# Filter stages of a spectral layer: products issued for two frequency groups at a time, with PSUM slots of their own

## The chip, the core and the metric

The kernel runs on one core of a Trainium2 chip. That core has a matrix engine (TensorE, PE in the profile), a vector engine (VectorE, DVE), an activation engine (ScalarE, ACT), a general engine (GpSimd, POOL) and a queue engine that only issues transfers (SyncE, SP). Each engine works through its own list of instructions in order; a semaphore holds an instruction until what it needs is done. Matrix products land in PSUM, everything else on the chip lies in SBUF, and transfers go over 16 shared DMA engines. The metric is the time of one execution on the device in microseconds (us), as the median of several runs.

## The reference

Four residual layers run one after the other on x of 2048 positions by 576 features: attention over a sliding window of 256, a spectral filter, the same attention again, the same filter again.

```python
def _B_ref(x, w_r, w_i):
    X = jnp.fft.rfft2(x, axes=(-2, -1))
    X = X * (w_r + 1j * w_i)
    return jnp.fft.irfft2(X, s=(S, D), axes=(-2, -1))

x = A_x
x = x + _A_ref(_layernorm(x, axis=-1), A_wqkv, A_wo)
x = x + _B_ref(_layernorm(x, axis=-1), B_w_r, B_w_i)
x = x + _A_ref(_layernorm(x, axis=-1), A_wqkv, A_wo)
x = x + _B_ref(_layernorm(x, axis=-1), B_w_r, B_w_i)
```

The change touches the spectral layers only, and of them the middle part: the last step of the forward transform over positions, the multiplication by the filter, and the first step of the way back.

## The kernel before

Transforms are matrix products. A spectral layer (`layer_b`) turns the features first, then the positions. The 2048 positions are split as 16 times 128, so the transform over positions has two steps with a transfer through DRAM between them (`yd[0]` on the way in, `yd[1]` on the way back). Between the two transfers stands the filter stage. It runs over 16 groups of frequencies, g = 0 to 15; a group is a tile of 128 rows with a real and an imaginary half of 290 columns each. Per group:

- `g0` (line 451) loads the rows of two groups from `yd[0]`, issued on SP (L455). `gw` (L458) loads the filter weights of two groups where they are not there yet (L196).
- `g1m` (L462) is the forward product: four matrix products of 128 rows by 64 columns (L467; group 0 has four more, L469) into a PSUM tile called `p2_g` (in the profile `p`). Two of them fill the two halves of the columns of the matrix array at the same time. Then DVE multiplies that tile by the weights twice (L475, L476), and POOL takes the difference and the sum of these products into the two halves of `uv` (L478, L479).
- `g2` (L481) is the backward product: four matrix products of 64 rows by 128 columns (L488) into a PSUM tile `pq`; here two products use the two halves of the rows at the same time. Group 0 uses all 128 rows. Then ACT copies the tile to SBUF as `both` (L510), POOL takes the difference of the first 192 columns (L513), and DVE takes the sum (L514) and the rest of the difference (L515). The result, called `ze` in odd groups and `eo` in even ones, is stored to `yd[1]` (L525). ACT issues that store for all even groups up to 12 and for the odd ones up to 7; SP issues it for 9, 11, 13 and 15, POOL for 14.

From group 11 on the rows that the first tiles of the next stage need also go straight from SBUF to SBUF (`rows`, L495, mostly on SP), and SP reads back what was stored for earlier groups (L519). The first tiles of the next stage take these; the later ones are loaded whole from `yd[1]` (`ly`, L545), which waits for the stores. The next stage starts with the products `pi` (L551).

The whole program is scheduled by hand: what is written first is issued first on each engine. `pipe` (L620) runs its stages with a lag each: at step t it calls every stage on group t minus its lag, in the order of the list. In the filter stage that list is `[(10, g2), (7, g1m), (2, gw), (0, g0)]`, so at step t the backward product of group t-10 is followed by the forward product of group t-7.

PSUM holds four tiles of this size, in two pools of the class `Banks` (L118). Tiles with the tag "mm" take three of the slots in turn (`turn`); the fourth has the tag "tp" and serves transposes (L234) and warm-up products (L331). `uv` has three buffers, `both` two, the products p1 two and p2 three.

The layer is built twice, for the second and the fourth layer of the reference; `first` is true in the second one's code. Behind the filter stage the first one runs some products for the weights of the next attention layer (`w1`, `w2`), the last one 36 warm-up products (L536).

Of the kernel before, what the change touches and what calls it, by code (L numbers as in the profile page):

```python
# [8 lines left out]
F32 = mybir.dt.float32  # L9
# [108 lines left out]
class Banks:  # L118
# [6 lines left out]
    def tile(self, shape, dtype, tag, name, bufs):  # L125
        if tag != "mm":
            return self.pools[tag not in self.lower].tile(shape, dtype, tag=tag, name=name, bufs=bufs)
        self.turn = (self.turn + 1) % 3
        return self.pools[self.turn == 2].tile(shape, dtype, tag=tag, name=name, bufs=2 if self.turn < 2 else 1)

def layer_b(tc, xf, dst, dcs, gc, ident, rh, rl, out, ga_d, fc_d, m2_d, w_d, wo_d, wo2_d, dram, nxt, share):

# [9 lines left out]
    with ExitStack() as stack:  # L142
# [4 lines left out]
        pp = Banks(tc, banks, "bps", ())  # L147
# [13 lines left out]
        def ld(n2, h=None):  # L161
            if n2 % 2 == 0 and n2 not in xs:
                x = pairs[n2 // 2 % 4].rearrange("p (a d) -> p a d", a=2)
                nc.sync.dma_start(x, xfv[:, n2:n2 + 2])
                for q in range(2):
                    xs[n2 + q] = x[:, q].rearrange("p (c f) -> p c f", c=2)
# [174 lines left out]
        def w1(j, h=None, pool=None):  # L341
            turned(pool or wp, 16 + j, wos[j], wos[j]["eo"], wos[j]["tl"], "mm" if j == 4 else "tp")
# [11 lines left out]
        if first:  # L354
# [39 lines left out]
            ps = pp.tile([128, 2, 512], F32, tag="mm", name="opsb", bufs=3)  # L394
# [65 lines left out]
                pre_w(g // 2)  # L460

        def g1m(g, h):  # L462
            ps = pp.tile([128, 2, 512], F32, tag="mm", name=f"p2_{g}", bufs=3)

            for c in range(2):
                for j in range(2):
                    T.matmul(ps[64 * j:64 * j + 64, c, 0:NF], fc[:, g, j, c], h["y"][:, j], start=True, stop=g > 0)  # L467
                    if g == 0:
                        T.matmul(ps[64 * j:64 * j + 64, c, 0:NF], fc[:, 16, j, c], h["y"][:, 1 - j], start=False, stop=True)  # L469
            if g in (11, 13):  # L470
                ld(g - 11)
            w = wt[g]
            p1 = tws[g % 2]
            p2 = wp.tile([128, 2, NF], F32, tag="tc", name=f"p2_{g}", bufs=3)
            V.tensor_mul(p1, ps[:, :, 0:NF], w)  # L475
            V.tensor_mul(p2, ps[:, :, 0:NF], w[:, ::-1])  # L476
            h["uv"] = uv = ip.tile([128, 2, NF], F32, tag="ta", name=f"uv{g}", bufs=3)
            P.tensor_sub(uv[:, 0], p1[:, 0], p1[:, 1])  # L478
            P.tensor_add(uv[:, 1], p2[:, 0], p2[:, 1])  # L479

        def g2(g, h):  # L481
            pq = pp.tile([128, 2, 512], F32, tag="mm", name=f"pq{g}", bufs=3)
            uv = h["uv"]

            for c in range(2):
                for j in range(2):
                    r = slice(64 * j, 64 * j + 64) if g else slice(0, 128)
                    T.matmul(pq[:, j, 0:NF], m2[r, g if g or j == 0 else 16, c], uv[r, c], start=c == 0, stop=c == 1)  # L488

            ye = wp.tile([128, 2, NF], F32, tag="ye", name=f"ze{g}", bufs=NY) if g % 2 else eos[2 + g // 2 % 2 if first else g // 2 % 4]  # L490
            both = ip.tile([128, 2, NF], F32, tag="both", name=f"both{g}", bufs=2)
            zs[g] = yef = ye.rearrange("p c f -> p (c f)")

            def rows(eng, n2, k):
                eng.dma_start(yis[n2][8 * k:8 * k + 8].rearrange("p c f -> p (c f)"), zs[k][8 * n2:8 * n2 + 8])  # L495

            if g == 15:
                A.copy(both[:, 1], pq[:, 1, 0:NF])
                V.tensor_add(ye[:, 0], pq[:, 0, 0:NF], both[:, 1])
                V.tensor_sub(ye[:, 1], pq[:, 0, 0:NF], both[:, 1])  # L500
                if first:
                    w1(3)
                else:
                    rows(nc.scalar, 2, 13)
                    rows(nc.scalar, 2, 14)
                for n2 in range(near):
                    rows(nc.sync, n2, 15)
                held.pop()()
            else:
                A.copy(both, pq[:, :, 0:NF])  # L510
                if near > 2 and g in (FG + 1, FG + 2):
                    rows(nc.scalar, 2, g - 1)
                P.tensor_sub(ye[:, 1, 0:SH], both[:, 0, 0:SH], both[:, 1, 0:SH])  # L513
                V.tensor_add(ye[:, 0], pq[:, 0, 0:NF], both[:, 1])  # L514
                V.tensor_sub(ye[:, 1, SH:NF], pq[:, 0, SH:NF], both[:, 1, SH:NF])  # L515
            if g in (FG - 1, FG + 1):
                lo, hi = (0, 8) if g < FG else (8, FG)
                for n2 in range(near):
                    nc.sync.dma_start(yis[n2][8 * lo:8 * hi].rearrange("p c f -> p (c f)"), yd[1][n2, lo:hi].rearrange("g i f -> (g i) f"))  # L519
            if FG <= g < 15:  # L520
                for n2 in range(2):
                    rows(P if g == 14 and n2 else nc.sync, n2, g)

            def store():
                (P if g == 14 else nc.scalar if g < 13 and (g < 8 or g % 2 == 0) else nc.sync).dma_start(yd[1][:, g], yef)  # L525
            if g == 13:
                held.append(store)
            else:
                store()

        zs, held = {}, []
        pipe(16, [(10, g2), (7, g1m), (2, gw), (0, g0)])
        if first:
            w2(3)
        else:
# [84 lines left out]
def pipe(n, stages, behind=None):  # L620
    hold = [dict() for _ in range(n)]
    for t in range(n + max(l for l, _ in stages)):
        for lag, fn in stages:
            if 0 <= t - lag < n:
                fn(t - lag, hold[t - lag])
        if behind:
            behind(t)
# [799 lines left out]
```

## Time and profile before

| | |
|---|---|
| median of 3 runs | 1382.74 us (1381.52 to 1386.3) |
| the profiled execution's own time | 1389.17 us |
| span of its profile | 1387.4 us |
| TensorE busy | 1342.3 us of the span |
| VectorE / ScalarE / GpSimd busy | 893.1 / 786.9 / 638.6 us |
| first filter stage, first forward to last backward product | 607.13 to 645.42 us |
| second filter stage | 1272.99 to 1315.42 us |

The profile shows one execution. A row of its timeline has the start in us from the beginning of the span, the time it took, the engine, the line of the kernel, the operation, out<-in by the names of the program, the shapes, and how many instructions were merged into the row; in brackets stands how long the engine had been idle and what released it. PEld is the loading of weights into the matrix array, and a small q behind an engine's name (ACTq, SPq) marks work of its instruction queue, the issuing of transfers above all. A matrix product of this type is two instructions, so four products read x8. A busy TensorE is not TensorE at its peak, since its products are pipelined and their ends modelled.

### The profile page before, as it was taken

The page shows a single profiled execution, that of the slowest core. Times are in us where ns is not written, and L with a number is a line of the kernel's source. Part 1 is how long each engine was busy: PE and PEld are TensorE (multiplying, and loading weights), DVE is VectorE, ACT ScalarE, POOL GpSimd, SP SyncE. Part 2 cuts the span into 40 slices and gives each one's busy share as a digit, 9 for nine tenths or more (in the row PEclk, how much of TensorE's full clock was granted, in tenths as well). Part 3 has the DMA queues.
Part 4 walks back from the last instruction along what each step waited for, and adds up shares of the span by engine and source line. Part 5 has one row for each costly group of instructions (what it writes and reads, how often), then busy time and mean ns, then how long its engine had stood idle before and what let it go on. Part 6 is the DMA issues. An engine that isn't in the chain of part 4 may idle for free.

```text
span 1387.4 us, 33518 instructions
## 1 busy us (share of the span) xinstructions
PE 1342.3 (97%) x11330; PEld 1000.8 (72%) x11330; DVE 893.1 (64%) x3045; ACT 786.9 (57%) x1980; POOL 638.6 (46%) x1139
## 2 busy tenths in 40 slices
PE   7999999999999999998999999999999999998998
PEld 7986666666665699975999975666666655897577
DVE  5417777877778266666673157777778783564745
ACT  5622777777778544443355316777777778463223
POOL 2257555555547533475211394455545457102711
PEclk9999999999999999999999999999999999999999
DMA  6746555655446457678773467555554565497874
GB/s 199 203 151 205 190 185 175 190 163 161 147 150 187 109 158 242 218 239 265 247 229 76 110 198 231 166 165 165 163 160 136 159 171 157 162 349 249 259 226 157
DMA packets 202015, 259.09 MB, mean 187 GB/s; under 512 B 104254, under 2 KB 109630, under 8 KB 201334
## 3 DMA queue, kind: packets, MB, share of 16 engines
q1 hardware_dynamic: 191350, 235.63, 55.4%
q10 hardware_dynamic: 8000, 15.63, 3.3%
q0 software_dynamic: 2496, 5.71, 1.5%
q8 instruction: 91, 1.49, 0.4%
q14 instruction: 78, 0.64, 0.1%
HBM read 156.26 MB, written 101.01 MB: 185 GB/s over the span
## 4 chain that ended last, share of the span: by engine, by line
PE 46%; DMA 4%; ACT 2%; DVE 1%; issue 1%; SPq 1%; POOL 0%; ACTq 0%; DVEq 0%; POOLq 0%
PE pj L1021 9%; PE S L1078 6%; PE U L1135 6%; PE vps L958 4%; PE ops L758 4%; PE po L251 4%; PE E L1115 3%; PE pq L488 2%; PE p L467 2%; PE pi L551 2%; PE tpo L1149 1%; ACT P L1116 1%; DMA ofree<-yd 1%; PE pz L289 1%; SPq L495 1%
## 5 line engine op out<-in xcount | busy, mean ns | idle before, releaser
L1080 DVE CUSTOM_DVE_ANT_0 jk<-S,mask 128x384 bf16<-128x384 f32 (+2 forms) x1024 | 490.4, 529 | 110.0 <-PE E L1115 59.0
L1116 ACT ACTIVATE P<-E 128x384 f32<-128x384 f32 (+2 forms) x1024 | 408.9, 476 | 121.9 <-PE E L1115 98.2
L1118 POOL TENSOR_SCALAR_AFFINE_SELECT P<-P 128x512 f32<-128x512 f32 x256 | 162.7, 635 | 280.4 <-ACT P L1116 260.4
L1078 PE MATMUL S<-ks,qs 63*128 63x384 f32 (+2 forms) x1024 | 269.7, 372 | 0.6 <-DVE m L1080 0.4
L1115 PE MATMUL E<-qs,ks 64*128 64x384 f32 (+2 forms) x1024 | 222.1, 372 | 3.0 <-ACT P L1116 2.5
L1078 PEld LDWEIGHTS S<-ks,qs 63*128 63x128 f32 x1024 | 140.7, 185 | 105.7 <-DVE m L1080 72.2
L1135 PE MATMUL U<-P,vq 128*19 128x128 f32 (+1 forms) x3840 | 187.8, 328 | 1.0 <-ACT us L1140 1.0
L1021 PE MATMUL pj<-xh,wqh 128*128 128x512 f32 x360 | 156.5, 435 | 2.8 <-DVE sg L1036 1.5
L1135 PEld LDWEIGHTS U<-P,vq 128*19 128x19 f32 x3840 | 95.7, 98 | 77.5 <-issue 21.3
L1121 POOL TENSOR_SCALAR_AFFINE_SELECT P<-P 128x512 f32<-128x512 f32 x224 | 142.4, 636 | 0.0
L1115 PEld LDWEIGHTS E<-qs,ks 64*128 64x128 f32 x1024 | 113.9, 185 | 17.0 <-ACT P L1116 7.9
L1021 PE MATMUL pj<-xh,wql 128*128 128x512 f32 x360 | 124.5, 419 | 0.3 <-POOL wql L648 0.3
L1021 PE MATMUL pj<-xl,wqh 128*128 128x512 f32 x288 | 122.2, 424 | 0.0
L758 PE MATMUL ops<-oroom 128*128 128x290 f32 (+1 forms) x812 | 116.5, 300 | 0.2
L758 PEld LDWEIGHTS ops<-oroom 128*128 128x128 f32 x812 | 111.6, 191 | 0.7 <-DVE ofree L781 0.7
L1021 PEld LDWEIGHTS pj<-xh,wqh 128*128 128x128 f32 x360 | 68.0, 189 | 34.1 <-issue 10.4
L1036 DVE TENSOR_TENSOR sg<-pj,sg 128x512 fp32r<-128x512 f32 x72 | 49.5, 687 | 57.8 <-ACT sg L1033 57.8
L1080 DVE DVE_READ_ACCUMULATOR2_ANT m<- 128x1 f32 x1024 | 85.2, 83 | 0.0
L1021 PEld LDWEIGHTS pj<-xh,wql 128*128 128x128 f32 x360 | 64.2, 189 | 20.9 <-issue 10.7
L1033 ACT CAST sg<-pj 128x512 fp32r<-128x512 f32 x72 | 42.2, 586 | 61.6 <-PE pj L1021 46.1
L243 ACT CAST et<-tp 128x512 fp32r<-128x512 f32 x53 | 31.2, 588 | 76.9 <-PE tp L239 76.1
L958 PE MATMUL vps<-wvh,xh 128*128 128x288 f32 x320 | 72.1, 307 | 0.1
(221 smaller groups left out, 2298.5 us busy)
## 6 DMA issues: line engine op xcount, KB each, us to landing
qk_d<-sg SPq DMA_DIRECT2D x56, 512.0 KB
qs<-qk_d SPq DMA_DIRECT2D x384, 72.0 KB
ks<-qk_d SPq DMA_DIRECT2D x348, 72.0 KB
v_d<-vt SPq DMA_DIRECT2D x32, 304.0 KB
vq<-v_d SPq DMA_DIRECT2D x16, 608.0 KB
wt<-in_w SPq DMA_DIRECT2D x16, 580.0 KB
ofree<-x SPq DMA_DIRECT2D x16, 580.0 KB
x<-ofree SPq DMA_DIRECT2D x32, 290.0 KB
```

What stands on the lines that cost most here:

```text
L251: T.matmul(ps[:, c, 0:NF], tail[r] if si == 4 else hl_(si), dcs[b // 2][r, b % 2], start=mi == si == 0, stop=si == 4)
L758: self.nc.tensor.matmul(self.ps[u][n][:, 0:self.n], x, self.w[p][:, (2 * wk + n) * self.n:(2 * wk + n + 1) * self.n], start=first and i == ...
L958: T.matmul(ps[:, n, 0:288], xT(xk, c), w[:, wk, n * 288:(n + 1) * 288], start=i == 0, stop=i == len(ks) - 1)
L1021: T.matmul(box["ps"].rearrange("r (n p) -> r n p", n=NT) if second else box["ps"], w[:, wk], x, start=s == 0, stop=s == len(ks) - 1)
L1036: V.tensor_sub(rest[:, 1], by, rest[:, 0].bitcast(F32))
L1078: T.matmul(ps[:, 0:N], q[b:b + 63, pair, i * 128:i * 128 + 128], k[b:b + 63, pair, lo:hi], start=True, stop=True)
L1080: V.tensor_tensor_reduce(out=jk[:, 0:N], in0=ps[:, 0:N], in1=mask[:, 384 - N:384], scale=1.0, scalar=-3e38, op0=ALU.add, op1=ALU.max, accu ...
L1115: T.matmul(ps[:, 0:nq], k[b:b + 64, pair, j * 128:j * 128 + 128], q[b:b + 64, pair, j * 128:j * 128 + nq], start=True, stop=True)
L1116: A.activation(p[:, hl_, 0:nq], ps[:, 0:nq], AF.Exp, scale=SC)
L1118: P.affine_select(out=p[:, :, 0:128], in_=p[:, :, 0:128], pattern=[[0, 4], [1, 128]], compare_op=ALU.is_ge, fill=0.0, base=0, channel_mult ...
L1121: P.affine_select(out=p[:, :, 256:384], in_=p[:, :, 256:384], pattern=[[0, 4], [-1, 128]], compare_op=ALU.is_gt, fill=0.0, base=0, channel ...
L1135: T.matmul(U[32 * h:32 * h + 19, (q0 % 4) * 128:(q0 % 4) * 128 + 128 * (q1 - q0)], vts[n][:, j, h], pt[n, j][:, h, (q0 - j) * 128:(q1 - j) ...
```

## The change

The forward products of groups 2m and 2m+1 are issued together, then the backward products of groups 2m-2 and 2m-1, and so on. The function `both_` does that: it is called on every group, does nothing for an even one, and for an odd one calls the stage for the even group before it and then for itself. The forward list stands at lag 7 and the backward one at lag 9, so that a pair's backward products come one pair of forward products after its own. Loads keep their lags (0 and 2), through `one`. The list of dictionaries `filt` replaces the one in `pipe`, since a call now works on two groups.

Each kind has PSUM slots of its own. `slot(k, name)` gives slot 0 or 1 of the first pool for forward products (`g % 2`), and of the second pool the "mm" slot for odd backward products and the "tp" slot for even ones (`3 - g % 2`). All four slots are thus used in the filter stage, where it was three before. Instructions, shapes and data are the same; only their order and their PSUM addresses change.

```diff
@@ class Banks
         self.turn = (self.turn + 1) % 3
-        return self.pools[self.turn == 2].tile(shape, dtype, tag=tag, name=name, bufs=2 if self.turn < 2 else 1)
+        return self.slot(self.turn, name)
+
+    def slot(self, k, name):
+        self.turn = min(k, 2)
+        return self.pools[k > 1].tile([128, 2, 512], F32, tag="tp" if k == 3 else "mm", name=name, bufs=2 if k < 2 else 1)
@@ g1m
-            ps = pp.tile([128, 2, 512], F32, tag="mm", name=f"p2_{g}", bufs=3)
+            ps = pp.slot(g % 2, f"p2_{g}")
@@ g2
-            pq = pp.tile([128, 2, 512], F32, tag="mm", name=f"pq{g}", bufs=3)
+            pq = pp.slot(3 - g % 2, f"pq{g}")
@@ the call of pipe
-        pipe(16, [(10, g2), (7, g1m), (2, gw), (0, g0)])
+        both_ = lambda fn: lambda g, h: [fn(k, filt[k]) for k in (g - 1, g)] if g % 2 else None
+        filt = [dict() for _ in range(16)]
+        one = lambda fn: lambda g, h: fn(g, filt[g])
+        pipe(16, [(7, both_(g1m)), (9, both_(g2)), (2, one(gw)), (0, one(g0))])
```

The lines of the changed kernel lie four further down (L467 is L471, L488 is L492, L510 is L514, L525 is L529). On TensorE the first filter stage begins so before; `p2_3` is the forward tile of group 3, `pq1` the backward tile of group 1, and the number behind the underscore only tells tiles apart:

```order
L467 MATMUL p2_2_9780<-ofree_6984,fc_8097 64x290 x4
L488 MATMUL pq0_9791<-uv0_9765,m2_8098 128x290 x4
L467 MATMUL p2_3_9802<-ofree_6984,fc_8097 64x290 x4
L488 MATMUL pq1_9814<-uv1_9776,m2_8098 128x290 x4
L467 MATMUL p2_4_9826<-ofree_6984,fc_8097 64x290 x4
L488 MATMUL pq2_9837<-uv2_9788,m2_8098 128x290 x4
L467 MATMUL p2_5_9848<-ofree_6984,fc_8097 64x290 x4
L488 MATMUL pq3_9862<-uv3_9810,m2_8098 128x290 x4
```

And now, from the same place:

```order
L471 MATMUL p2_2_9780<-ofree_6984,fc_8097 64x290 x4
L471 MATMUL p2_3_9791<-ofree_6984,fc_8097 64x290 x4
L492 MATMUL pq0_9802<-uv0_9765,m2_8098 128x290 x4
L492 MATMUL pq1_9813<-uv1_9776,m2_8098 128x290 x4
L471 MATMUL p2_4_9826<-ofree_6984,fc_8097 64x290 x4
L471 MATMUL p2_5_9837<-ofree_6984,fc_8097 64x290 x4
L492 MATMUL pq2_9848<-uv2_9788,m2_8098 128x290 x4
L492 MATMUL pq3_9859<-uv3_9799,m2_8098 128x290 x4
```

Forward and backward blocks alternated one by one; now they alternate by twos. VectorE has the same order: the four products of a pair of groups, then sum and difference of the even backward tile, then of the odd one.

On GpSimd the same stretch, with the semaphores that each instruction waits for in brackets, was this before (`uv` are the sums of the products, `ze` and `eo` the differences of the backward tiles):

```order
L478 TENSOR_TENSOR uv4_9834<-ofree_6984 128x290 [waits DVE_49]
L479 TENSOR_TENSOR uv4_9834<-p2_4_9831 128x290 [waits DVE_49]
L513 TENSOR_TENSOR eo3_8102<-both2_9842 128x192 [waits Activation_49]
L478 TENSOR_TENSOR uv5_9856<-ofree_6984 128x290 [waits DVE_49]
L479 TENSOR_TENSOR uv5_9856<-p2_5_9853 128x290 [waits DVE_49]
L513 TENSOR_TENSOR ze3_9867<-both3_9868 128x192 [waits DMASW3_49,DMASW4_49,DMASW2_49,Activation_49]
```

Now it is this:

```order
L482 TENSOR_TENSOR uv4_9834<-ofree_6984 128x290 [waits DVE_49]
L483 TENSOR_TENSOR uv4_9834<-p2_4_9831 128x290 [waits DVE_49]
L482 TENSOR_TENSOR uv5_9845<-ofree_6984 128x290 [waits DVE_49,PE_49]
L483 TENSOR_TENSOR uv5_9845<-p2_5_9842 128x290 [waits DVE_49]
L517 TENSOR_TENSOR eo3_8102<-both2_9853 128x192 [waits Activation_49]
L517 TENSOR_TENSOR ze3_9864<-both3_9865 128x192 [waits DMASW3_49,DMASW4_49,DMASW2_49,Activation_49]
```

The difference of the even backward tile has moved behind the sums of the odd group, and those wait for TensorE as well: with three buffers, `uv5` lies where `uv2` lay, which the backward product of group 2 reads.

On ScalarE nothing has moved. Copies of the backward tiles and the stores of the results alternate as they did; in the changed kernel these rows read:

```order
L514 COPY both0_9807<-pq0_9802 128x580 [waits DVE_49,PE_49,Activation_49]
L529 DMA yd1_8081<-eo2_8101 16x8x580 [waits DMAHW0_49,DVE_49,Pool_49]
L514 COPY both1_9819<-pq1_9813 128x580 [waits PE_49,Activation_49]
L529 DMA yd1_8081<-ze1_9818 16x8x580 [waits DMAHW1_49,DVE_49,Pool_49]
L514 COPY both2_9853<-pq2_9848 128x580 [waits PE_49,Activation_49]
L529 DMA yd1_8081<-eo3_8102 16x8x580 [waits DMAHW4_49,DVE_49,Pool_49]
```

The store of an even group waits for VectorE and GpSimd and stands ahead of the copy of the odd group; what has changed is where the instructions that it waits for stand on their engines.

## The prediction

> **What bounds the kernel now.** I read the page's busy times first, then the busy times by stage, then the timelines of the engines in the filter stages, then the chain of waits behind them.
>
> ```profile
> PE 1342.3 (97%) x11330; PEld 1000.8 (72%) x11330; DVE 893.1 (64%) x3045; ACT 786.9 (57%) x1980; POOL 638.6 (46%) x1139
> 617.10:640.17 23.07, 23.07 (x162) 11.75 (x162) 19.63 (x41) 6.43 (x10) 18.47 (x31) 1.00 0.92 315
> ```
>
> The second row is ten groups of the first filter stage: length, busy us of PE, PEld, DVE, ACT and POOL, granted clock, DMA share, GB/s. PE never stops, DVE is busy for 19.63 of 23.07 us, POOL for 18.47. PE is the bound, the two behind it are close.
>
> ```profile
> 609.14 2.17 PE L467 MATMUL p<-ofree,fc 128*64 128x290 f32 x16
> 611.25 2.22 PE L488 MATMUL pq<-uv,m 128*128 128x290 f32 x8
> 613.40 1.20 PE L467 MATMUL p<-ofree,fc 128*64 128x290 f32 x8
> 614.53 1.25 PE L488 MATMUL pq<-uv,m 64*128 64x290 f32 x8
> 615.71 1.20 PE L467 MATMUL p<-ofree,fc 128*64 128x290 f32 x8
> ...
> 611.41 0.75 DVE L476 TENSOR_TENSOR p<-p,wt 128x580 f32<-128x580 f32 x1
> 614.77 0.75 DVE L475 TENSOR_TENSOR ofree<-p,wt 128x580 f32<-128x580 f32 x1
> 615.44 0.75 DVE L476 TENSOR_TENSOR p<-p,wt 128x580 f32<-128x580 f32 x1
> 616.55 0.46 DVE L514 TENSOR_TENSOR ze<-pq,both 128x290 f32<-128x290 f32 x1 [0.36 <-ACT both L510]
> 617.10 0.75 DVE L475 TENSOR_TENSOR ofree<-p,wt 128x580 f32<-128x580 f32 x1
> 640.17 0.75 DVE L475 TENSOR_TENSOR ofree<-p,wt 128x580 f32<-128x580 f32 x1
> 646.39 0.45 DVE L500 TENSOR_TENSOR ze<-pq,both 128x290 f32<-128x290 f32 x1
> ...
> 616.27 0.70 POOL L479 TENSOR_TENSOR uv<-p 128x290 f32<-128x290 f32 x1
> 616.92 0.52 POOL L513 TENSOR_TENSOR ze<-both 128x192 f32<-128x192 f32 x1
> ...
> 615.88 0.64 ACT L510 COPY both<-pq 128x580 f32<-128x580 f32 x1 [1.69 <-PE pq L488]
> 617.48 0.58 ACTq L525 DMA_DIRECT2D yd<-ze  x1
> 638.27 0.53 ACTq L525 DMA_DIRECT2D yd<-eo  x1
> ```
>
> See the steps. On PE, a forward block alone takes 1.13 us (613.40 to 614.53), a backward one 1.18 (to 615.71). On DVE the products start 0.67 apart, and from the first product of one group (617.10) to that of the group ten later (640.17) it is 23.07 us: 2.307 a group, 4.61 a pair. The others follow at fixed distances, which I use below.
>
> **The change: what it removes.** Two forward blocks in a row took 2.11 us (609.14 to 611.25), 0.15 less than twice 1.13, so each change of kind costs PE about 0.15. A stage has 27 such changes before and 13 after: 14 times 0.15 is 2.1 us, 4.2 for both stages. This is a gain only while PE is the bound.
>
> **What it adds: a loop through ACT's queue.** ACT's list is unchanged: copy of the even backward tile, its store, copy of the odd tile. The store waits for DVE and POOL. These now do the pair's four products and four half sums first. If the odd copy can't pass the waiting store, it waits for all that, and DVE, in order, has the odd tile's sum ahead of the next pair's products. Whether a waiting transfer holds a copy is seen at the end of the second stage, where ACT has one such transfer more:
>
> ```profile
> 644.54 0.64 ACT L510 COPY both<-pq 128x580 f32<-128x580 f32 x1 [0.34 <-PE pq L488]
> ...
> 1314.45 0.69 ACTq L495 DMA_DIRECT2D ofree<-eo  x1
> 1315.24 0.64 ACT L510 COPY both<-pq 128x580 f32<-128x580 f32 x1 [1.03 <-PE pq L488]
> 1315.78 0.41 ACT L498 COPY both<-pq 128x290 f32<-128x290 f32 x1
> ```
>
> In the first stage the copy of group 14 comes after 0.34 us of idling; in the second a transfer stands between, is issued until 1315.14, and the copy comes 0.10 later, after 1.03. It was held, through the issue too.
>
> [...]
>
> Now the loop, from the first product of pair (2m, 2m+1) at time M. The fourth product starts at M+2.00 (3 times 0.67). POOL's second half sum of the odd group starts 0.83 later (615.44 to 616.27): M+2.83. Its difference of the even tile follows 0.65 later (to 616.92) and lasts 0.52: M+4.00. The store starts 0.04 later (617.48), takes 0.53 (row 638.27), and the copy follows after 0.10: M+4.67. DVE's sum starts 0.67 after the copy (615.88 to 616.55), the next products 0.55 after that (to 617.10): **M+5.89**. Against 4.61 that is +1.28 a pair. PE needs 4.61 less two changes of kind, 4.31, so it idles 1.6 us in each pair; DVE's own work is 3.8 (4 times 0.67, twice 0.55), and neither is the bound. What is late is always the odd copy.
>
> The first stage in three parts. *Opening:* forward tiles have two slots, so group 3's waits until group 1's second product has ended, 611.41 plus 0.75, and starts at 612.25 instead of behind pq0. Plus 1.13 and the 2.15 of pq0 (611.25 to 613.40), seen 0.17 later (615.71 to 615.88), it is 615.7. The odd sum `uv3` lies in `uv0`'s buffer, so it starts then; 0.67 + 0.65 + 0.52 + 0.04 + 0.53 + 0.10 + 0.67 + 0.55 later group 4's products start: 619.4, where it was 617.10, **+2.3**. In later pairs the buffer of `uv` costs nothing: the backward product that reads it is over well before M. *Loop:* five steps from pair (4, 5) to (14, 15), 5 times 1.28, **+6.4**. *Closing:* with M the last pair's, the tile of group 13 is read out at M+5.9. Only then its slot takes the last backward block (1.18, seen 0.17 later); the copy of half a tile (0.41, row 1315.78) and two sums (0.46 and 0.45, a little overlapped) end at M+8.5. Before it was 640.17 to 646.84, 6.67: **+1.8**. So the last result stands 10.5 us later, at 657.3.
>
> What of this reaches the end is set behind the stage:
>
> ```profile
> 644.08 0.75 SPq L519 DMA_DIRECT2D ofree<-yd  x2
> 648.51 1.30 SPq L495 DMA_DIRECT2D ofree<-ze  x2
> 650.49 3.95 DMA yd<-ze
> 654.58 3.65 DMA ofree<-yd
> 658.36 2.27 PE pi L551 x4
> 664.86 0.98 PE pi L551 x4
> 668.38 0.98 PE pi L551 x4
> ```
>
> SP works through row transfers without a pause from 644.08, released by the landing of group 10's store (issued 638.27, 5.81 before). It comes to those of group 15 at 648.51, 1.67 after they were ready. Then come the last stores, their landing (3.95), a load (3.65), and PE goes on at 658.36. After the change the rows are ready at 657.3; SP is free then too (group 10's store at 647.0, plus 5.81, plus the 4.43 from 644.08 to 648.51). The rows go out at 657.4 instead of 648.51, and PE goes on **8.9** later. Against it stands the clock:
>
> ```profile
> 131.74:135.15 3.41, 1.94 (x10) 0.97 (x9) 1.86 (x6) 1.85 (x4) 1.76 (x3) 0.99 0.54 173
> 653.98:657.39 3.41, 1.49 (x13) 1.28 (x11) 0.69 (x1) 1.50 (x3) 0.57 (x3) 0.99 0.77 230
> 1271.80:1275.21 3.41, 2.22 (x18) 1.69 (x20) 0.00 (x0) 0.00 (x0) 0.00 (x0) 1.00 0.38 97
> ```
>
> After a stretch of 3.41 us with PE busy for 1.49, PE's tiles ran slow: 6.50 us from 658.36 to the next `pi`, where the following take 3.52, a loss of 3.0. After the change PE leaves the stage 10.6 later (656.0 for 645.42) and this wait ends 8.9 later, so the stretch before it is fuller and the clock may hold: 0 to -3.0. I take **-1.5**, the middle, since nothing here decides it. First stage: +7.4, between 5.9 and 8.9.
>
> The second stage:
>
> ```profile
> 1280.58 2.90 PE L488 MATMUL pq<-uv,m 128*128 128x290 f32 x8
> 1283.41 0.95 PE L467 MATMUL p<-ofree,fc 128*64 128x290 f32 x6
> 1287.11 0.75 DVE L475 TENSOR_TENSOR ofree<-p,wt 128x580 f32<-128x580 f32 x1
> 1308.26 0.53 ACTq L525 DMA_DIRECT2D yd<-eo  x1
> 1315.21 1.46 SPq L519 DMA_DIRECT2D ofree<-yd  x2
> 1316.83 0.45 DVE L500 TENSOR_TENSOR ze<-pq,both 128x290 f32<-128x290 f32 x1
> 1320.75 1.30 SPq L495 DMA_DIRECT2D ofree<-ze  x2
> ```
>
> Its loads come late, so no slot delays group 3; it starts in pq0's place at 1280.58. That block took 2.83 us instead of 2.15, 0.68 of a slow clock that now falls on group 3. So 1.13 + 0.68 + 2.15 + 0.17 and the same 3.73 of steps: 1288.4, **+1.3** against 1287.11. With 5 steps and the closing the last result stands at 1288.4 + 29.45 + 8.5 = 1326.4, where it was 1317.28. But SP came to its rows at 1320.75 only. If they now wait for nothing else, it is +5.7. If group 10's store, now at 1316.05, needs 6.95 us to free SP as before (1308.26 to 1315.21) and SP then the same 5.54, it is 1328.5, +7.8. With the first stage's 5.81 it is +6.7, which I take, since the slower loop asks less of the DMA engines (0.92 busy now).
>
> Sum: 7.4 + 6.7 = **14.1 us**, between 11.6 and 16.7. On the profiled execution's 1389.17 (span 1387.4) that is 1403.3, 1.0% more. That execution lay 0.5% above the median of the runs; on the median of 1382.74 it is **1396.8**. Loads, weights and x are issued on SP for pairs three ahead and have more time than now: nothing.
>
> **Rivals.** *Copies pass waiting stores.* Then PE stays the bound and the fewer changes of kind give 4.2 us. The opening takes back 1.0 in the first stage (groups 2 and 3 wait 0.7 and 0.3 for their slots, which without them would start at 610.1 and 611.9 instead of 610.8 and 612.25), and SP behind the stages, late already, swallows a part: between 0 and -3.2, I say -2, 1380.7. It decides from the point where an odd copy starts within 0.2 us of its backward block's end. Row 1315.24 speaks against it, the shorter forward blocks for it. [...]
>
> *A copy passes the store's issue but not its wait.* It would then start 0.63 earlier (0.53 + 0.10), in 7 pairs of each stage: 8.8 less, +5.3, 1388.0. The same row is against it, since there the copy waited for the issue too.
>
> *The clock falls in the loop.* The rows above say that 1.94 busy of 3.41 lost the clock and 2.22 kept it. In the loop PE is busy 4.31 of 5.89, and around its longest gap (1.1 and 0.3) about 2.0 of 3.41, between them. One fall costs 1.7 us at most and hides in the 1.6 idle of a pair; lasting, 8.6 a pair, 2.7 more in 12 pairs: +33 on top, 1429. At half speed PE is busy all the time, which speaks against lasting.
>
> *The ends swallow more.* If the landings and loads behind the stages (7.6 us in the first, about as much in the second) get shorter by 2 each, and both lower bounds hold, it is 11.6 - 4 = +7.6, 1390.3.
>
> **How the numbers follow.** The likeliest has 0.71, with 1394.3 to 1399.4 as its own range; the two rivals on ACT's queue 0.08 each, the clock 0.05, the ends 0.08. The range reaches from 1390, the ends' case, to 1401, the upper bound with a little of the clock's. A measurement of this kernel tells 0.3% (4 us) from nothing. Faster by more comes only from the first rival's upper half, 0.04; no change from its rest and some of the second, 0.05; slower is 0.91.
>
> **What would show it.** In the profile after: odd copies on ACT start 0.10 behind the store of the even group, 4.67 after the pair's first product; those first products lie 5.89 apart; PE idles about 1.6 a pair, ended by ACT, DVE or POOL; two blocks of a kind take 2.1. The stages last about 49 and 52 us instead of 38.3 and 42.4. Wrong it would be if odd copies start right behind their products on PE, or if the distance is near 4.3.

## The result, and the profile after

The changed kernel takes 1404.33 us (median of 5 runs, 1401.2 to 1405.13), the kernel before 1381.92 (median of 5, 1379.59 to 1386.3): a ratio of 1.0148, 95% interval 1.0132 to 1.0164. A second measurement, shown below, gave 1.0135 (1.0109 to 1.0162). It is slower, as forecast, but by more than forecast: 1396.8 was a ratio of 1.0102, and the upper end of the range, 1401, one of 1.0132.

The two profiled executions took 1389.17 and 1405.13 us, 16.0 apart; 14.1 was forecast for them. Where it went is read in the same order as before: busy times, then the stretch of five pairs in each filter stage (length, busy us of PE, PEld, DVE, ACT and POOL, granted clock, DMA share, GB/s).

```profile
PE 1343.9 (96%) x11330; PEld 1002.3 (71%) x11330; DVE 891.6 (64%) x3045; ACT 786.5 (56%) x1980; POOL 639.2 (46%) x1139
618.72:648.43 29.71, 24.39 (x166) 13.21 (x162) 19.17 (x41) 6.97 (x11) 18.63 (x31) 1.00 0.75 229
1296.02:1325.72 29.70, 24.45 (x166) 13.16 (x162) 19.18 (x41) 6.97 (x11) 18.62 (x31) 1.00 0.76 231
```

The work is the same, the length is not: ten groups take 29.71 us where they took 23.07. TensorE is busy for 24.4 of it, and no engine for more. That is the mark of a loop from engine to engine, in which each waits for the next. TensorE idles in two gaps, 1.08 us a pair (0.19 and 0.89). Here is one turn of it, by the timelines of PE, DVE, POOL and ACT (start, time taken; in brackets the idle time before and what ended it):

```profile
620.24 1.20 PE L471 MATMUL p<-ofree,fc 128*64 128x290 f32 x8
621.62 1.20 PE L471 MATMUL p<-ofree,fc 128*64 128x290 f32 x8 [0.19 <-DVE p L480]
622.75 1.25 PE L492 MATMUL pq<-uv,m 64*128 64x290 f32 x8
624.89 1.25 PE L492 MATMUL pq<-uv,m 64*128 64x290 f32 x8 [0.89 <-DVE ze L519]
...
618.72 0.75 DVE L479 TENSOR_TENSOR ofree<-p,wt 128x580 f32<-128x580 f32 x1
620.72 0.75 DVE L480 TENSOR_TENSOR p<-p,wt 128x580 f32<-128x580 f32 x1
624.12 0.46 DVE L518 TENSOR_TENSOR ze<-pq,both 128x290 f32<-128x290 f32 x1 [2.11 <-ACT both L514]
624.66 0.75 DVE L479 TENSOR_TENSOR ofree<-p,wt 128x580 f32<-128x580 f32 x1
...
621.61 0.70 POOL L483 TENSOR_TENSOR uv<-p 128x290 f32<-128x290 f32 x1
622.26 0.53 POOL L517 TENSOR_TENSOR eo<-both 128x192 f32<-128x192 f32 x1
...
622.82 0.53 ACTq L529 DMA_DIRECT2D yd<-eo  x1
623.44 0.64 ACT L514 COPY both<-pq 128x580 f32<-128x580 f32 x1 [3.24 <-PE p L471]
```

From M = 618.72: fourth product M+2.00, second half sum of the odd group M+2.89, difference of the even tile M+3.54 to M+4.07, store M+4.10, copy of the odd tile M+4.72, its sum M+5.40, next products M+5.94. Forecast were 2.00, 2.83, 3.48, 4.00, 4.04, 4.67, 5.34 and 5.89. The copy begins 0.09 behind the store's issue, after ScalarE had idled 3.24, and the backward block that it reads had ended by 620.28 (618.05 plus 2.23), 3.16 us before. Whether the store ahead of it is what holds it is tried below.

The closing of the first stage (PE, then DVE):

```profile
648.66 1.25 PE L492 MATMUL pq<-uv,m 64*128 64x290 f32 x8 [0.89 <-ACT both L514]
651.87 2.31 PE L492 MATMUL pq<-uv,m 64*128 64x290 f32 x8 [1.96 <-DVE eo L519]
654.61 2.30 PE L492 MATMUL pq<-uv,m 64*128 64x290 f32 x8 [0.43 <-DVE ze L519]
...
648.43 0.75 DVE L479 TENSOR_TENSOR ofree<-p,wt 128x580 f32<-128x580 f32 x1
654.21 0.25 DVE L519 TENSOR_TENSOR ze<-pq,both 128x98 f32<-128x98 f32 x1
657.80 0.45 DVE L504 TENSOR_TENSOR ze<-pq,both 128x290 f32<-128x290 f32 x1
```

The last two backward blocks took 2.3 us each instead of 1.25: in the gap before them, for the even tile's read-out, TensorE's clock had fallen to half. In the second stage it fell later, and only the last block was slow (1329.16 and 1331.90 below). The windows show it as the granted clock, the third figure from the end:

```profile
647.96:651.38 3.42, 1.25 (x8) 0.78 (x8) 3.42 (x7) 0.56 (x1) 2.58 (x5) 1.00 0.40 107
651.38:658.20 6.82, 5.90 (x22) 3.74 (x22) 2.37 (x8) 1.68 (x3) 3.24 (x6) 0.50 0.55 136
658.20:661.61 3.41, 2.73 (x21) 2.58 (x21) 0.74 (x2) 1.26 (x3) 0.00 (x0) 1.00 0.44 108
1327.21:1330.63 3.42, 1.25 (x8) 0.78 (x8) 1.80 (x4) 0.18 (x1) 2.54 (x5) 1.00 0.57 143
```

The clock fell at 651.38 and 1330.63, each time behind 3.41 us with TensorE busy for 1.25. In this profile and in the first one of before the changes of the granted clock lie whole multiples of 3.413 us apart (here 651.38, 658.20 and 1330.63; before 135.10, 657.34 and 664.17), but where they fall in the program differs between the two.

Behind the first stage and at the end of the second (PE, DVE, SP; `warm` are the 36 warm-up products):

```profile
668.00 1.22 PE L558 MATMUL pi<-ofree,ga 128*128 128x290 f32 x4 [1.59 <-DMA ofree<-yd]
671.60 1.14 PE L558 MATMUL pi<-ofree,ga 128*128 128x290 f32 x4
675.13 1.14 PE L558 MATMUL pi<-ofree,ga 128*128 128x290 f32 x4
1329.16 1.25 PE L492 MATMUL pq<-uv,m 64*128 64x290 f32 x8 [1.96 <-DVE eo L519]
1331.90 2.30 PE L492 MATMUL pq<-uv,m 64*128 64x290 f32 x8 [1.49 <-DVE ze L519]
1334.13 6.54 PE L337 MATMUL warm<-dc 128*128 128x290 f32 x36
1340.51 2.12 PE L558 MATMUL pi<-ofree,ga 128*128 128x290 f32 x8
1351.68 1.14 PE L558 MATMUL pi<-ofree,ga 128*128 128x290 f32 x4
...
1335.09 0.45 DVE L504 TENSOR_TENSOR ze<-pq,both 128x290 f32<-128x290 f32 x1
...
655.92 0.62 SPq L499 DMA_DIRECT2D ofree<-eo  x1
658.28 1.30 SPq L499 DMA_DIRECT2D ofree<-ze  x2
1333.22 0.62 SPq L499 DMA_DIRECT2D ofree<-eo  x1
1335.57 1.98 SPq L499 DMA_DIRECT2D ofree<-ze  x3
```

In both stages SP idles ahead of the last rows (658.28, 1335.57) and goes on right behind the last result (658.25, 1335.54). Before, it was SP that came late: 1.67 us after the rows were ready in the first stage. In the first stage the clock then held: 3.60 from 668.00 to the next `pi`, where it was 6.3 before (658.36 to 664.70). In the second the warm-up products began at half clock, took 6.54 us instead of 5.08 and pushed `pi` to 1340.51.

To compare executions I measure each stage from its first forward product: to the end of its last result, and to the fourth row of `pi` products, where TensorE runs undisturbed again (675.13 and 1351.68 here). This table is read from the same rows of all profiles; "pair" is the distance between the first products of two pairs, the mean of five:

| profile | pair | 1st stage: last result | 4th `pi` | 2nd stage: last result | 4th `pi` | ratio to before |
|---|---|---|---|---|---|---|
| before | 4.61 | 39.7 | 61.1 | 44.3 | 62.7 | |
| before, second profile | 4.61 | 39.7 | 60.4 | 43.2 | 60.8 | 0.9990 (0.9980 to 1.0001) |
| changed | 5.94 | 51.9 | 68.8 | 55.0 | 71.1 | 1.0148 (1.0132 to 1.0164) |
| changed, second profile | 5.94 | 51.9 | 68.7 | 53.4 | 69.6 | 1.0135 (1.0109 to 1.0162) |
| copies first | 4.26 | 39.9 | 59.4 | 43.8 | 61.8 | 1.0008 (0.9992 to 1.0024) |
| difference ahead | 5.20 | 47.0 | 63.9 | 48.6 | 63.9 | 1.0060 (1.0041 to 1.0080) |
| slots alone | 4.61 | 41.3 | 59.9 | 43.5 | 60.1 | 0.9998 (0.9985 to 1.0011) |
| order alone | 5.94 | 48.4 | 68.1 | 51.1 | 68.5 | 1.0103 (1.0077 to 1.0129) |
| late slots | 5.94 | 49.5 | 70.1 | 52.7 | 71.1 | 1.0121 (1.0097 to 1.0146) |
| all three | 4.26 | 39.4 | 60.5 | 43.3 | 61.6 | 1.0009 (0.9994 to 1.0024) |
| ends | 4.26 | 39.7 | 60.6 | 44.7 | 62.3 | 1.0008 (0.9996 to 1.0020) |
| before with ends | 4.61 | 39.7 | 58.1 | 43.0 | 60.3 | 0.9986 (0.9974 to 0.9999) |

Changed less before is 7.7 + 8.4 = 16.1 us by the first pair of profiles and 8.3 + 8.8 = 17.1 by the second. What lies outside these two stretches (span less both) is 1263.6 and 1263.5 in the first pair, and 1262.0 to 1266.3 over all twelve profiles, whatever the kernel. So the loss in these executions is in the two filter stages and what follows each.

### The profile page after: what moved, and what is told of

The parts are those of the page before. It is cut to its first block, busy times and chain, and to the rows that moved or that the text cites. A ratio compares the mean times of both kernels' runs of the same rounds, so it can differ in the third digit from the quotient of the medians.

```text
span 1403.4 us, 33528 instructions
## 1 busy us (share of the span) xinstructions
PE 1343.9 (96%) x11330; PEld 1002.3 (71%) x11330; DVE 891.6 (64%) x3045; ACT 786.5 (56%) x1980; POOL 639.2 (46%) x1139
## 4 chain that ended last, share of the span: by engine, by line
PE 72%; DMA 8%; POOL 4%; ACT 3%; DVE 3%; issue 3%; SPq 2%; ACTq 1%; DVEq 0%; POOLq 0%
PE pj L1028 16%; PE S L1085 11%; PE U L1142 10%; PE ops L765 7%; PE E L1122 5%; PE vps L965 4%; PE po L255 4%; PE pf L255 2%; PE tpo L1156 2%; PE pi L558 2%; ACT P L1123 2%; DMA ofree<-yd 2%; PE pz L293 2%; DMA qs<-mt 1%; DMA ks<-qk_d 1%
## 5 line engine op out<-in xcount | busy, mean ns | idle before, releaser
L1043 DVE TENSOR_TENSOR sg<-pj,sg 128x512 fp32r<-128x512 f32 x72 | 49.5, 687 | 58.3 <-ACT sg L1040 58.3
L1028 PEld LDWEIGHTS pj<-xh,wql 128*128 128x128 f32 x360 | 64.2, 189 | 20.9 <-issue 10.7
L1040 ACT CAST sg<-pj 128x512 fp32r<-128x512 f32 x72 | 42.1, 585 | 61.6 <-PE pj L1028 51.8
L247 ACT CAST et<-tp 128x512 fp32r<-128x512 f32 x53 | 31.1, 587 | 71.4 <-PE tp L243 71.2
```

The source lines that it names most:

```text
L1028: T.matmul(box["ps"].rearrange("r (n p) -> r n p", n=NT) if second else box["ps"], w[:, wk], x, start=s == 0, stop=s == len(ks) - 1)
L1043: V.tensor_sub(rest[:, 1], by, rest[:, 0].bitcast(F32))
```

## The experiments

**Copies first.** Theory: the store ahead of the odd copy closes the loop. Rival: pairing starves TensorE by itself.

```diff
                 A.copy(both, pq[:, :, 0:NF])
+                if late:
+                    late.pop()()
...
             if g == 13:
                 held.append(store)
+            elif g % 2 == 0 and g < 13:
+                late.append(store)
             else:
                 store()
```

> The changed kernel, with one instruction moved on ScalarE: the store of an even group up to 12 is issued behind the copy of the odd group instead of ahead of it. ScalarE's queue theory: the odd copy no longer waits for GpSimd's difference, the loop is gone, and TensorE is the bound again at 4.31 us a pair (4.61 less two changes of kind). The first products of a pair lie 4.3 to 4.5 apart instead of 5.94, and the last result of the first stage comes 39 to 41 us after the stage's start instead of 51.9; the time falls from 1404 to between 1378 and 1384. Rival, the pairing by itself starves TensorE (two forward slots, three buffers of uv, the order on GpSimd): the distance stays above 5 and the time above 1390. Rival, the copies were never held and the time went elsewhere: nothing changes, 1404.

Measured: 1388.73 us against 1387.1 of before, a ratio of 1.0008. The profile, one pair (PE, ACT) and the store of group 10:

```profile
618.79 2.17 PE L471 MATMUL p<-ofree,fc 128*64 128x290 f32 x16
620.90 2.23 PE L492 MATMUL pq<-uv,m 64*128 64x290 f32 x16
...
617.99 0.64 ACT L514 COPY both<-pq 128x580 f32<-128x580 f32 x1 [2.65 <-DVE ofree L479]
618.97 0.64 ACT L514 COPY both<-pq 128x580 f32<-128x580 f32 x1 [0.34 <-PE pq L492]
620.02 0.53 ACTq L531 DMA_DIRECT2D yd<-eo  x1
637.08 0.53 ACTq L531 DMA_DIRECT2D yd<-eo  x1
```

TensorE has no idle time left, the odd copy waits for nothing but its block, and a pair takes 4.26. One instruction moved in one queue takes nearly all of the loss back: the loop went through ScalarE's queue. The 0.35 us between 4.61 and 4.26 is the gain of two fewer changes of kind in a pair. Yet the kernel isn't faster than before, and the time missed what was expected (1378 to 1384): those bounds stood on before's 1382 us, and before measured 1387.1 beside this run; besides, they took for granted that the loop's gain reaches the time. From the last group's first product to the last result it takes 6.3 and 8.6 us, 4.4 and 5.0 in the second profile of before.

**Difference ahead.** GpSimd's order alone; ScalarE's queue stays as in the changed kernel.

```diff
+        def g1s(g, h):
+            uv, (p1, p2) = h["uv"], h["p"]
             P.tensor_sub(uv[:, 0], p1[:, 0], p1[:, 1])
             P.tensor_add(uv[:, 1], p2[:, 0], p2[:, 1])
...
+                do(g1m, g - 1)
+                do(g1s, g - 1)
+                do(g1m, g)
+                do(g2, g - 3)
+                do(g1s, g)
+                do(g2, g - 2)
```

> The changed kernel, with GpSimd's list alone in another order: the difference of the even backward tile stands ahead of the odd group's two sums instead of behind them. ScalarE's list is as in the changed kernel, store ahead of the odd copy. ScalarE's queue theory: the store then waits for VectorE's part of the even tile, which ends 0.77 before GpSimd's did (1299.31 against 1300.09), so the odd copy, the odd sum and the next products come 0.77 earlier: 5.17 us between the first products of two pairs instead of 5.94. With 5 steps, an opening and a closing in each stage that is about 5 us a stage, 1394 (1391 to 1397). Rival, the loop goes through PSUM slots, buffers or VectorE's own order: the distance stays at 5.94 and the time at 1404.

Measured: 1395.92 us, a ratio of 1.0060 where the changed kernel had 1.0135 to 1.0148. DVE, POOL and ACT:

```profile
624.67 0.75 DVE L479 TENSOR_TENSOR ofree<-p,wt 128x580 f32<-128x580 f32 x1
629.88 0.75 DVE L479 TENSOR_TENSOR ofree<-p,wt 128x580 f32<-128x580 f32 x1
...
626.83 0.53 POOL L521 TENSOR_TENSOR eo<-both 128x192 f32<-128x192 f32 x1
...
628.04 0.53 ACTq L533 DMA_DIRECT2D yd<-eo  x1
628.66 0.64 ACT L518 COPY both<-pq 128x580 f32<-128x580 f32 x1 [2.56 <-POOL uv L487]
```

The store stands at M+3.37 instead of M+4.10, and the distance falls by as much, from 5.94 to 5.20 on average. So the store's wait sets the loop, and in the changed kernel what it waits for last is GpSimd's difference. The time fell about as said: 0.0075 to 0.0088 of ratio is 10 to 12 us.

**Slots alone, order alone.** The two halves of the change.

```diff
-        pipe(16, [(7, both_(g1m)), (9, both_(g2)), (2, one(gw)), (0, one(g0))])
+        pipe(16, [(10, one(g2)), (7, one(g1m)), (2, one(gw)), (0, one(g0))])
```

> Half of the change: the slots of the changed kernel (two for forward products, one for odd and one for even backward products), with the order of before, one backward and one forward block in turn. If the order is what costs: the pairs lie 4.61 us apart as before, and the time is that of before within 0.3% (1378 to 1386). If the slots cost by themselves (a forward tile must wait for its own kind's slot): TensorE idles in the stage, and the time is 1388 or more.

```diff
-            ps = pp.slot(g % 2, f"p2_{g}")
+            ps = pp.tile([128, 2, 512], F32, tag="mm", name=f"p2_{g}", bufs=3)
...
-            pq = pp.slot(3 - g % 2, f"pq{g}")
+            pq = pp.tile([128, 2, 512], F32, tag="mm", name=f"pq{g}", bufs=3)
```

> The other half of the change: the pairs' order, with forward and backward tiles taking the three slots of before in turn. ScalarE's queue theory: the loop runs through the order only, so the distance between pairs is 5.9 to 6.0 us as in the changed kernel, and the ratio to before 1.012 to 1.018. Rival, one slot of its own for each kind matters: with three slots in turn the even backward block has to wait for the odd tile's read-out of the pair before, and if that adds to the loop the distance is over 6.3 and the ratio over 1.02; if on the other hand the slots of their own were the cost, the distance falls towards 4.6.

Slots alone: 1388.14 us, 0.9998, pairs of 4.61; nothing in the time. (The bounds of 1386 and 1388 were put on the earlier, lower base; before measured 1387.1 beside it.) Order alone: 1401.55 us, 1.0103, pairs of 5.94, the whole loop. The ratio came out below what was expected. With three slots in turn two things are cheaper: group 3's forward block doesn't wait for a slot of its kind (the last group's first product stands 42.3 us from the stage's start instead of 43.4), and the last four backward blocks follow each other without the gap of 1.96, at 4.90 us for the four:

```profile
647.11 4.90 PE L492 MATMUL pq<-uv,m 64*128 64x290 f32 x32 [1.14 <-DVE ze L519]
```

So under the order by pairs the slots of their own cost 3.5 us of the 12.2 by which the first stage's last result is late (51.9 less 48.4); under the order of before they cost 1.6 (41.3 against 39.7). Little of the 3.5 is seen at the fourth `pi`: 68.1 against 68.8. Whether that explains the whole of the lower ratio isn't shown.

**Late slots.** The closing alone.

```diff
-            pq = pp.slot(3 - g % 2, f"pq{g}")
+            pq = pp.slot(g % 2 if g > 13 else 3 - g % 2, f"pq{g}")
```

> The changed kernel, with the backward tiles of groups 14 and 15 in the two forward slots, which nobody uses any more by then. It tests the closing. Slot theory: the two last blocks no longer wait for the read-out of groups 12 and 13; with M the first product of the last pair, block 14 can start when its half sums are ready (M+2.2), block 15 at M+3.6 instead of M+6.18, TensorE's gap of 1.96 goes and with it the half clock of the last block. What is left is ScalarE's odd copy (M+4.7) and VectorE's six operations behind it: the last result at about M+7.7 instead of M+9.82, 2 us earlier in each stage, and in the second stage the 36 warm-up products run at full clock. 3 to 6 us less than the changed kernel, a ratio of 1.010 to 1.013. Rival, the closing is set by the copies alone: under 1 us in a stage and no change in the time.

Measured: 1403.52 us, 1.0121 against 1.0135 for the changed kernel beside it; the intervals overlap. PE, at the end of the first and of the second stage:

```profile
649.25 4.17 PE L492 MATMUL pq<-uv,m 64*128 64x290 f32 x24 [0.89 <-DVE ze L519]
668.28 1.54 PE L558 MATMUL pi<-ofree,ga 128*128 128x290 f32 x4 [3.01 <-DMA ofree<-yd]
673.50 1.14 PE L558 MATMUL pi<-ofree,ga 128*128 128x290 f32 x4
1339.11 4.21 PE L558 MATMUL pi<-ofree,ga 128*128 128x290 f32 x8 [3.24 <-DMA ofree<-ze]
```

Half of the expectation held. The last blocks run at full clock, and the last results come 2.4 and 2.3 us earlier. But the time is only 1.6 us less where 3 to 6 were expected, and in this profile nothing arrives: the fourth `pi` stands at 70.1 and 71.1. TensorE now waits longer for its rows, its clock falls in that wait or right behind it (5.22 us from 668.28 to the next `pi` instead of 3.60; 4.21 for the first two `pi` of the second stage instead of 2.12), and what the result gained the slow products lose. Late result and full clock, or early result and half clock: in these profiles the ends come out alike.

**All three, and the ends.** Do the pairs pay once the loop and the closing are mended? First, copies first and late slots together, with ScalarE's row transfers of groups 11 and 12 in the second stage moved behind the copies of 13 and 15.

```diff
-                if near > 2 and g in (FG + 1, FG + 2):
-                    rows(nc.scalar, 2, g - 1)
+                if near > 2 and g == 13:
+                    rows(nc.scalar, 2, 11)
...
-                    rows(nc.scalar, 2, 13)
-                    rows(nc.scalar, 2, 14)
+                    for k in (12, 13, 14):
+                        rows(nc.scalar, 2, k)
```

> Three edits of the changed kernel together: even stores behind the odd copies (as in the run with the copies first, which came to before's time), the tiles of groups 14 and 15 in the forward slots, and in the second stage ScalarE's row transfer of group 11 behind the copy of 13 and that of 12 behind the last copy. The loop is then 4.27 us a pair, below before's 4.61, and the closing, which took 6.3 and 8.6 us from the last product to the last result with the copies first against 4.4 and 5.0 before, should fall to 4 to 5.5. If SyncE's queue behind the stages lets it through, 2 to 4 us less than before, a ratio of 0.997 to 0.999; if SyncE's row transfers, ready at their own pace, decide the ends, the ratio is 0.999 to 1.001.

Measured: 1389.21 against 1386.67, a ratio of 1.0009. The closing was still 5.8 and 8.0 us, where 4 to 5.5 were expected. Then two edits behind the stage, on this kernel and on before (the store of 13 is no longer held back behind the rows of 15, either):

```diff
-                (P if g == 14 else nc.scalar if g < 13 and (g < 8 or g % 2 == 0) else nc.sync).dma_start(yd[1][:, g], yef)
+                (P if g > 12 else nc.scalar if g < 13 and (g < 8 or g % 2 == 0) else nc.sync).dma_start(yd[1][:, g], yef)
...
-            warm(36)
+            warm(60)
```

> The three edits together once more, and behind the stage two others: the stores of groups 13 and 15 are issued by GpSimd as soon as these are ready, not by SyncE behind the row transfers, and behind the second stage stand 60 warm-up products instead of 36. It tests what swallowed the gains of the stage. If it is the chain from SyncE's last store over its landing (about 4 us) to the load of the third tile, and TensorE's half clock behind a gap, then that load can start about 2 us earlier in each stage and the first pi products run at full clock: 60.5 and 61.6 us from the stage's start to the fourth pi row become 58 to 59.5 each, and the ratio to before 0.996 to 0.999. If SyncE's row transfers or the DMA engines themselves are the limit, nothing changes: 0.999 to 1.002.

> The kernel before with the same two edits behind the stage and no other: stores of 13 and 15 from GpSimd, 60 warm-up products. It tells what the pairs' order is worth once the ends let a gain through. If the ends are as said, this is faster than before by 1 to 4 us, a ratio of 0.997 to 0.999, and the kernel with pairs is faster than this one by what its loop saves, 1 to 3 us. If the two come out alike, the order by pairs is worth nothing even without its loop through ScalarE's queue.

Measured: 1388.77 us with pairs, 1.0008; 1385.61 without, 0.9986 (0.9974 to 0.9999). The second is the only version here whose whole interval lies below 1, and that barely: the kernel before, measured once more against itself, came out at 0.9990 (0.9980 to 1.0001). The kernel with pairs, expected 1 to 3 us ahead of it, is 3.2 us behind. In the first stage the loads do start earlier, but TensorE's first `pi` row waits for other rows and starts 45.3 us from the stage's start, with pairs, and 45.5 without. It then takes 4.21 us with pairs, at half clock, and 2.19 without, at full clock; the 2.5 us between the fourth rows (60.6 and 58.1) come behind it. SP, second stage of the kernel with pairs and ends:

```profile
1317.16 1.37 SPq L524 DMA_DIRECT2D ofree<-yd  x3
1318.63 1.34 SPq L499 DMA_DIRECT2D ofree<-eo  x2
1320.07 1.29 SPq L499 DMA_DIRECT2D ofree<-ze  x2
1321.48 0.78 SPq L499 DMA_DIRECT2D ofree<-eo  x1
1322.35 2.57 SPq L499 DMA_DIRECT2D ofree<-ze  x3
```

SP works without a pause from 1317.16 on, so the rows that `pi` needs are set by when it begins, not by the last result (1319.86). In the first stage of before and of the kernel with the copies first it begins when the store of group 10 has landed. With the copies first that store is issued 32.1 us from the stage's start (637.08 less 604.94) and SP begins at 37.8; before these were 31.1 (638.27 less 607.13) and 37.0. Counted from group 4's first product the store stands at 21.2 us in both: what the faster loop gains up to there is taken by its later place, behind two forward blocks and two copies. The 1.0 that is left is the longer opening (11.0 us instead of 10.0 to group 4's first product). So the gain of the pairs, 0.35 us each, isn't seen on the path that goes through this store. That this path is what keeps the gain from the time is argued from the rows, not tried, and which of the waits holds the second stage wasn't tried either.

**Both kernels once more.**

> The kernel before once more, for a second profiled execution. The first one's own time, 1389.2, lay 7 us above the median of the runs, and that of the changed kernel only 1 above its median; that is where most of the miss in the predicted difference could lie. If the 7 us were a disturbance of that one execution, the second has a span of 1378 to 1383, and the comparison by stretches shows where the first lost them; the two filter stages keep 38.3 and 42.4 us within 0.5. If a profiled execution of before is always that long, the span is again about 1387.

> The changed kernel once more, for a second profiled execution of it. From its start to the fourth row of pi products the first filter stage took 68.8 us and the second 71.1; in the two profiled executions of before these were 61.1 and 62.7, then 60.4 and 60.8. If before's first execution was the odd one, mainly in its second stage, this run repeats 68.8 and 71.1 within 1 us, and its ratio is again 1.013 to 1.017. If the changed kernel's stages vary as much, the second stage comes out 1.5 us or more off.

Before: 1385.5 us (12 runs, 1382.84 to 1388.94), the profiled execution 1388.94. Changed: 1405.13 (5 runs), the profiled one 1405.13. First stages repeat within 0.7 us. The second stage is 1.9 us shorter in before's second profile and 1.5 in the changed kernel's, both for 1.1 to 1.6 in the last result: its opening varies from one execution to the next, in both kernels. So neither expectation fits whole. The first profile of before wasn't odd in itself. The stages of two profiles compare to 2 us or so, whole executions less well: over the twelve profiles here the profiled execution lay between 4.3 us below and 7.3 us above the median of its kernel's runs.

## Where the prediction held, and which steps failed

The direction and the mechanism held; the size did not. 1396.8 us was forecast, 1401 at most, and 1404.33 measured, 7.5 more than the likeliest. Two steps failed. In the sum, the closing was too short, because the half clock was left out of it: with what followed it in the second stage, the sum came out 1.9 us low (14.1 for 16.0 between the profiles). The other 5.6 are the base: a sum worked out on one profiled execution was put on the median of before's runs. What lies behind that second difference stays open.

- *The loop through ScalarE's queue*: right, in place and size. 5.94 us a pair for 5.89, each step within 0.07 us; taking the store away from ahead of the copy ends it, moving the store by 0.73 moves it by 0.74. One sign was off: TensorE idles 1.08 a pair, not 1.6, for in the loop two blocks of a kind don't run together (620.24 to 622.75 is 2.51, not 2.1); the second waits for VectorE. The loop doesn't go through TensorE, so this cost nothing.
- *The gain of fewer changes of kind*: there, 0.35 for two changes where 0.30 was put, but only where the loop is gone.
- *Opening*: +2.4 and +1.3 (618.72 less 606.35 against 617.10 less 607.13; 1296.02 less 1280.57 against 1287.11 less 1272.99), forecast +2.3 and +1.3. The second is in part luck: that opening varies by 1.3 and 1.6 us between two profiles of one kernel. *Five steps*: +6.6, forecast +6.4.
- *Closing*: the term that was mis-sized. M+9.82 in both stages, forecast M+8.5. The tile of group 13 was read out at M+6.03 instead of M+5.9, the last block, which takes its slot, started at M+6.18, and it ran at half clock: 2.30 where 1.18 was put. The prediction had weighed the clock for the loop, whose gaps it survived (granted 1.00 in both stretches), and for the wait behind the stage, but not for the gap in the closing, which is longer than any in the loop: 1.96 us. With that gap gone the last blocks ran at full clock and the last result stood at M+7.4 and M+7.6 (late slots).
- *Behind the first stage*: forecast +10.5 at the last result, +8.9 when PE goes on, +7.4 in the end. Measured +12.2, +10.4 (61.65 against 51.23 from the start) and +7.7. The clock gave back 2.7 rather than 1.5, which covered most of the closing's miss.
- *Second stage*: here the sum failed, 6.7 (up to 7.8) forecast, 8.4 measured (8.8 in the second pair of profiles). The last result is 10.7 later for 9.1, 1.3 of it the closing. SP had no work left to delay the rows, so the 1.0 added for that wasn't there; but from the rows on another 1.1 was lost. The warm-up products, which began at the half clock that the closing left behind, took 1.46 longer than before; that this is the cause is argued, since no run changed them alone.
- *The sum*: 16.1 in the profiles for 14.1, inside the 11.6 to 16.7.
- *The base*: the rest of the miss. The prediction put the profiles' difference on the median of before, as if both profiles stood alike to their medians. They don't: before's two lay 7.3 and 3.4 us above theirs, the changed kernel's 0.8 and 0.0. The medians are 22.4 and 18.5 apart, the profiled executions 16.0 and 16.2. In which part of the unprofiled runs the other 2 to 6 us lie no run here shows; it stays open.
- *The rivals*: copies passing waiting stores, or their issue, didn't occur: the odd copy began 0.09 behind the issue. The clock didn't fall in the loop (1.00 in both stretches). But the two rows that this was argued from give no threshold: counted in steps of 3.41 us back from the changes at 651.38 and 1330.63, TensorE was busy for at least 2.4 of each step in the loop, not about 2.0, and one stretch of 1.54 (650.18 to 653.59 in before with ends, its place an estimate) kept the clock too. The ends didn't swallow more than forecast in the second stage, and in the first only by the clock. The first rival's time is still worth a look: the kernel with copies first is the world it described, and its -2 us came out at a ratio of 1.0008 (0.9992 to 1.0024), no gain; the closing and the store of group 10 had been left out.

## What to carry to other kernels

Here a copy waited for the store ahead of it in ScalarE's queue, with 3.24 us of idling before it, and with the store behind the copy a pair took 4.26 us instead of 5.94: when work is regrouped, list for each queue what an instruction now waits for and what stands behind, and try the issues behind the copies. The faster loop, 4.26 us a pair for 4.61 before, was worth only what reached the transfer that the next stage waits for; by the rows of the first stage, that was the store of group 10 of 16, and it came no earlier (21.2 us from group 4's first product in both). And a base taken from one profiled execution carries that execution's luck, up to 7.3 us of 1389 here: two of them, or the ratio to several runs, are worth having before a forecast of 1%.

## What was unexpected of the hardware

Behind a gap of 1.96 us, with TensorE busy for 1.25 of 3.41, the granted clock stood at 0.50 for 6.8 us, while gaps of 0.89 and 0.19 in each pair of 5.94 us left it at 1.00. How empty a stretch is didn't decide it alone: this one, of before with ends, is emptier, and the clock was kept in it and behind it (the first `pi` row, at 652.05, took 2.19 us):

```profile
648.61:652.02 3.41, 0.56 (x6) 0.35 (x4) 0.69 (x1) 1.44 (x3) 0.00 (x0) 1.00 0.88 272
```

That profile's clock changed at 1271.42 and 1274.83 (blocks of four products start 0.51 us apart up to 1271.43 and 0.97 apart behind it). Counted back from there in steps of 3.413 us, which is an estimate from the profiles of before and changed, it could have changed at 650.18 and 653.59. The stretch lies across the first of these points, and TensorE was busy for 2.40 of the 3.41 us ahead of it and for 1.54 of those behind it. Whether that place is what kept the clock isn't shown. And in the one profile with late slots the last result came 2.3 us earlier in the second stage and 2.4 in the first, and the fourth `pi` no earlier in either, behind slow products (5.22 us for 3.60, 4.21 for 2.12).
